# A fused attention and two-layer feed-forward kernel on one core: when the sums of x are built, by which engine, and in which slices weight blocks are converted

## Chip, cores and metric

The kernel runs on one core of a Trainium2 chip. The metric is the device time of one execution in microseconds (us). Three runs of the kernel before stand beside one profiled execution.

## What is computed

Local attention (a window of 32 positions, in half of the heads with a stride of 4) gives a matrix `x` of 2304 tokens by 512. Two feed-forward layers follow it:

```python
def reference(**kwargs):
    attn_out = _attn_ref(**attn_kwargs)          # 4 x 8 heads x 576 x 64
    x = np.ascontiguousarray(attn_out.transpose(0, 2, 1, 3)).reshape(B * S, H * D)
    x = _moe_ref(x=x, **moe_kwargs)              # silu(x @ w_gate) * (x @ w_val) @ w_out, d_ff 1536
    return _moe2_ref(x=x, **moe2_kwargs)         # ((x @ w1) * (x @ w2)) @ w3 @ w_out, d_ff 1024
```

The weights come as 64-bit floats. The kernel rebuilds 32-bit floats from their words, and splits every number into a high and a low part, so that one product is three matmuls (high by high, high by low, low by high).

## The kernel before, in words

**Slices and groups.** The two layers are cut into 20 slices `c` of 128 hidden columns: slices 0 to 11 (`NFT` = 12) are layer one, 12 to 19 layer two. In each slice the tokens are worked off in five groups `g`, four of 512 tokens and one of 256. A step (c, g) is written (8, 2) below. `steps` (L938) walks through them.

**One step.** `up_mm` (L564) forms two products into PSUM banks `pa` and `pb`, 24 matmuls. `up_act` makes `ga` of `pa` on ScalarE (L576 with SiLU in layer one, L578 a copy in layer two), `pr` = `pb` by `ga` on VectorE (L637), its high part `sh` on ScalarE (L644) and its low part `sl` on GpSimd (L645). Then comes `down` of the step *before*: 12 matmuls of `sh` and `sl` with the third weight block into banks `po0` to `po3`, and VectorE adds these to the sums `y` (L730, layer one) or `o` (L728, L730, layer two). So `sh` and `sl` of a step are wanted on TensorE one whole step after its `up` products have ended. A matmul covers 512 columns; group 4 has half the columns, or half the matmuls.

**Jobs.** What stands between two steps is set by a table, `plan(c)` (L210 on), and run by `follow` (L925). A job `("w", c+1, j)` converts weight block j of the next slice: five operations on VectorE (L126 to L136, `to_f32`), a cast on ScalarE (L199, `whi`), a subtraction on GpSimd (L200, `wlo`). `("wo", j, 0)` does the same for one of the eight blocks of the last matrix, `("w3", f, half)` for half a block of `w3`, with a transpose. `("fold", f)` is 24 matmuls that multiply `w3` and the last matrix into one matrix, which goes to memory and comes back as blocks `("fw", c, 2)`, which need a cast and a subtraction but no conversion. Loads run ahead by two jobs on SyncE's queue (`run_jobs`, L258).

**Pairs.** In the slices of `PAIRS` (L205) the groups 0 and 1 are done in one go by `pair` (L865): seven half products in place of eight, so 42 matmuls in place of 48. For that it needs four sums of blocks of `x`, and sums of weights. `t_sums` (L814) builds the former once for each layer, as a generator that does one part at each `("T",)`: additions of 128x1024 on VectorE (L816, L819), each result cast on ScalarE (`split`, L811) and its low part subtracted on GpSimd (L812). The first of them takes the place of part of `x` itself and must wait for the last plain product of group 1. `s_sums` (L855) builds the sums of weights slice by slice. The buffers of the sums of x take the room of those of the fold, so all folds come first.

**Slice 11** is the last of layer one. Its `down1` adds in another order of tokens (`total`, L751), casts the result to the next layer's `x_hi` on ScalarE (L755) and subtracts `x_lo` on GpSimd (L756), group by group, while the products of slice 11 and 12 go on.

Of the kernel before, what the change touches and what calls it, by code (L numbers as in the profile page):

```python
# [23 lines left out]
KW = QB + WINDOW  # L24
NIDLE = 8
GFILL = 4
PAIR0, PAIR1 = 9, 13
SQ = 32
NEG = -1.0e9

# [5 lines left out]
def attention_ffn_kernel(  # L36
# [14 lines left out]
    nc = tc.nc  # L51
    B, H, S, D = q.shape
# [7 lines left out]
    NFT = FF // P  # L60
    NF2 = FF2 // P
# [5 lines left out]
    while t0 < NT:  # L67
        n = min(512, NT - t0)
# [24 lines left out]
    for _ in range(NIDLE):  # L93
# [113 lines left out]
    def order_of(c):  # L207
        return ["pair", 2, 3, 4] if c in PAIRS else [0, 1, 2, 3, 4]

    def plan(c):  # L210

        res = {g: [] for g in order_of(c)[:1] + ["mid"] + order_of(c)[1:]}
        if c in PAIRS:

            res["pair"] = [("w" if c < NFT else "fw", c, 2)]
        if c + 1 == NCH:
            return res
        w0, w1, w2 = (("w", c + 1, j) for j in range(3))
        if c + 1 >= NFT:
            w2 = ("fw", c + 1, 2)  # L220
        if c == 0:

            res[4] = [w2]
        elif c < PAIR0 - 1:
            f = 2 * (c - 4)
            if f < 0:
                res[0], res[3] = [w0, w1], [w2]
                for n, g in enumerate((1, 2, 4)):
                    if 3 * c - 3 + n < NJ:
                        res[g] = [("wo", 3 * c - 3 + n, 0)]  # L230
            else:
                res = {0: [("w3", f, 1), w0], 1: [("fold", f), ("w3", f + 1, 0), w1], 2: [("w3", f + 1, 1)],
                       3: [("fold", f + 1), w2], 4: []}
            if f >= -2:
                res[4].append(("w3", f + 2, 0) if f + 2 < NF2 else ("T", c + 1))
        elif c + 1 == PAIR1 or c + 1 == PAIR0:
            res = {0: [("T",), w0], 1: [("T",), w1, ("T",)], 2: [("T",)], 3: [("S", c + 1)], 4: []}
        elif c == NFT - 1:
            res.update({"mid": [w0], 2: [w1], 4: [("T", c + 1), w2]})
        else:  # L240
            res.update({"mid": [w0], 2: [w1], 3: [("S", c + 1)]})
        return res
# [533 lines left out]
    def down(c, g):  # L776
        (down1 if c < NFT else down2)(c, g)
# [31 lines left out]
    def split(dst, t):  # L809
        hi, lo = dst  # L810
        nc.scalar.copy(out=hi, in_=t)  # L811
        nc.gpsimd.tensor_tensor(out=lo, in0=t, in1=f32(hi), op=ALU.subtract)  # L812

    def t_sums(layer):  # L814
        def sub(dst, a, b):
            nc.vector.tensor_tensor(out=dst, in0=a, in1=b, op=ALU.subtract)  # L816

        def add(dst, a, b):
            nc.vector.tensor_tensor(out=dst, in0=a, in1=b, op=ALU.add)  # L819

        if not pair_pool:
            fp.release()
            pair_pool.append(ctx.enter_context(tc.tile_pool(name="pp", bufs=1, side="right")))
        (h11, l11), (h21, l21), (h12, l12), (h22, l22) = (tuple(f32(t) for t in half(g, k))
                                                          for g in range(2) for k in range(2))
        for i in (2, 3, 4):
            xs[i] = tuple(pair_pool[0].tile([P, HK, 512], F32R, tag=f"T{i}{n}", name=f"T{i}{n}{layer}", bufs=1)
                          for n in "hl")
        t1, d = temp("Sf", f"t1_{layer}"), temp("Sh", f"d1_{layer}")
        sub(t1, h12, h11)  # L830
        sub(d, l12, l11)
        add(t1, t1, d)
        yield
        t3, d = temp("Sh", f"t3_{layer}"), temp("Sl", f"d3_{layer}")
        sub(t3, h22, h12)
        sub(d, l22, l12)
        add(t3, t3, d)
        split(xs[3], t3)
        yield
        split(half(1, 0), t1)  # L840
        yield
        t2 = temp("Sl", f"t2_{layer}")
        sub(t2, h22, t1)
        add(t2, t2, l22)
        split(xs[2], t2)
        yield
        t4 = temp("Sh", f"t4_{layer}")
        sub(t4, h21, t2)
        add(t4, t4, l21)
        split(xs[4], t4)  # L850
        yield

    ss = {}
# [11 lines left out]
    def pair(c, between):  # L865
        whi, wlo = whl[c]
        shi, slo = ss.pop(c)

        def weights(j, k):
            return tuple(w[:, j * PW + k * HK * P:j * PW + (k + 1) * HK * P] for w in (whi, wlo))  # L870

        def sums(i):
            return shi[:, i - 1], slo[:, i - 1]

        def product(pt, a, b, first, last):
            terms = [(i, j, kk) for kk in range(HK) for i, j in ((0, 0), (1, 0), (0, 1))]
# [24 lines left out]
        product(y, weights(0, 1), half(0, 1), True, True)
        gate0 = snap("ca", x)
        add(gate0, y)
        job = plan(c)["pair"]
        for _ in range(5 if job and job[0][0] != "fw" else 0):
            next(running)
        product(x, sums(2), xs[2], False, False)
        product(z, sums(1), half(1, 0), True, False)
        gate1 = snap("cb", x)
        silu(gate0)  # L910
        product(x, sums(3), xs[3], False, False)
        val1 = snap("cc", x)
        add(val1, z)
        between()
        product(x, weights(1, 1), xs[4], False, True)
        prod(0, gate0, x)
        next_job()
        product(z, sums(4), half(1, 1), False, True)
        add(gate1, z)
        silu(gate1)  # L920
        prod(1, gate1, val1)

    sums_of_x = []

    def follow(c, g):  # L925
        for what, *args in plan(c)[g]:
            if what == "fold":
                fold_mm(*args)
            elif what == "S":
                s_sums(*args)  # L930
            elif what == "T":
                if args:
                    sums_of_x.append(t_sums(*args))
                next(sums_of_x[-1])
            else:
                next_job()

# [2 lines left out]
    for n, (c, g) in enumerate(steps):  # L940
        if g == "pair":
            pair(c, lambda: down(*behind.pop()))
            behind = [(c, 0), (c, 1)]
        elif len(behind) == 2:
            gate, val = bank("pb", f"pb{c}_{g}", 2), bank("pa", f"pa{c}_{g}", 2)
            upp[c, g] = gate, val
            for j, pt in enumerate((gate, val)):
                for _ in up_product(c, g, j, pt):
                    pass
                if j == 0:  # L950
                    down(*behind.pop(0))
# [12 lines left out]
        if g != "pair":
            follow(c, g)
# [31 lines left out]
```

## Time and profile before

| | us |
|---|---|
| median of three runs (902.17 to 905.53) | 902.73 |
| the profiled execution, its own time | 902.85 |
| its span | 901.1 |
| TensorE (PE) busy | 865.7 (96%) |
| VectorE (DVE) busy | 685.4 (76%) |
| ScalarE (ACT) busy | 274.4 (30%) |
| GpSimd (POOL) busy | 367.9 (41%) |

The profiled execution lies 1.75 us over its span and 0.12 us over the median. In a timeline row stand the start in us, the duration in us (from first to last where a row merges several), the engine, the line of the kernel, the operation, output and inputs, their sizes, the count, and in brackets the idle time before it with what ended that. Matmul records follow each other in steps shorter than their durations, since matmuls are pipelined. A few matmul records are missing.

### The profile page before, as it was taken

Reading aid. Unit: us, or ns where it says so; the run is one execution under the profiler, and the core shown is the slowest. Engines: PE = TensorE matmul, PEld = TensorE weight load, DVE = VectorE, ACT = ScalarE, POOL = GpSimd, SP = SyncE. Lnnn points to the kernel's source line nnn. Section 1 sums busy time; section 2 is a strip of 40 time slices with the busy share of each in tenths; the row PEclk is TensorE's granted clock in tenths of the full one; section 3 lists DMA queues with packets and bytes.
Section 4 is the critical chain, followed back from the end, with each engine's and each line's share of the span. In section 5 each row is a group of like instructions: output and inputs, shape, how many; then the busy total and the mean of one; then the engine's idle time right before and its main releaser. Section 6 shows DMA issues by size and latency. Waiting matters only on the chain. (4 is left out here: it accounts for less than half of the span.)

```text
span 901.1 us, 13592 instructions
## 1 busy us (share of the span) xinstructions
PE 865.7 (96%) x5132; PEld 714.8 (79%) x5132; DVE 685.4 (76%) x1150; ACT 274.4 (30%) x545; POOL 367.9 (41%) x332
## 2 busy tenths in 40 slices
PE   8899999999999999999989999897999999999998
PEld 5678788888888888888868888675787888878886
DVE  6898978878888878787787777898675665756744
ACT  6778422222222222222122323332222222222221
POOL 7676523333333332322253333785343334322431
PEclk9999999999999999999989999998999999999999
DMA  8988312222233333332110111101010110110014
GB/s 193 220 194 170 119 47 71 95 71 94 73 79 87 93 84 95 82 89 82 62 44 24 47 50 33 47 13 47 1 59 12 47 39 22 58 36 23 13 46 166
DMA packets 107857, 65.91 MB, mean 73 GB/s; under 512 B 71952, under 2 KB 100880, under 8 KB 107792
## 3 DMA queue, kind: packets, MB, share of 16 engines
q1 hardware_dynamic: 107248, 64.78, 26.7%
q8 instruction: 41, 0.67, 0.3%
q10 hardware_dynamic: 544, 0.26, 0.1%
q14 instruction: 24, 0.20, 0.1%
HBM read 58.20 MB, written 6.82 MB: 72 GB/s over the span
## 5 line engine op out<-in xcount | busy, mean ns | idle before, releaser
L645 POOL TENSOR_TENSOR sl<-pr,sh 128x512 fp32r<-128x512 f32 (+1 forms) x98 | 115.6, 1180 | 171.6 <-ACT sh L644 171.6
L200 POOL TENSOR_TENSOR wlo<-val_w,whi 128x512 fp32r<-128x512 f32 x52 | 67.8, 1304 | 167.2 <-ACT whi L199 165.2
L730 DVE TENSOR_TENSOR y<-po,y 128x512 f32<-128x512 f32 (+1 forms) x200 | 114.5, 629 | 1.0 <-PE po L744 1.0
L637 DVE TENSOR_TENSOR pr<-pb,ga 128x512 f32<-128x512 f32 (+1 forms) x68 | 41.7, 613 | 96.0 <-ACT ga L576 44.3
L560 PE MATMUL pa<-x_hi,whi 128*128 128x512 f32 (+1 forms) x312 | 112.6, 364 | 0.0
L560 PE MATMUL pa<-x_hi,wlo 128*128 128x512 f32 (+1 forms) x312 | 112.3, 363 | 0.0
L560 PE MATMUL pb<-x_hi,whi 128*128 128x512 f32 (+1 forms) x312 | 112.1, 362 | 0.0
L560 PE MATMUL pb<-x_hi,wlo 128*128 128x512 f32 (+1 forms) x312 | 112.0, 362 | 0.0
L560 PE MATMUL pb<-x_lo,whi 128*128 128x512 f32 (+1 forms) x312 | 100.5, 362 | 0.0
L560 PE MATMUL pa<-x_lo,whi 128*128 128x512 f32 (+1 forms) x312 | 100.3, 362 | 0.0
L744 PE MATMUL po<-sh,whi 128*128 128x512 f32 (+1 forms) x240 | 90.3, 376 | 7.7 <-DVE total L751 3.7
L644 ACT CAST sh<-pr 128x512 fp32r<-128x512 f32 (+1 forms) x98 | 56.6, 577 | 129.0 <-DVE pr L637 79.2
L744 PE MATMUL po<-sl,whi 128*128 128x512 f32 (+1 forms) x240 | 90.8, 378 | 1.7 <-POOL sl L645 1.7
L730 DVE TENSOR_TENSOR o<-po,o 128x512 f32<-128x512 f32 x126 | 80.9, 684 | 14.0 <-PE po L771 14.0
L744 PE MATMUL po<-sh,wlo 128*128 128x512 f32 (+1 forms) x240 | 89.6, 373 | 0.0
L199 ACT CAST whi<-val_w 128x512 fp32r<-128x512 f32 x52 | 32.2, 620 | 187.6 <-DVE val_w L136 187.6
L560 PEld LDWEIGHTS pa<-x_hi,whi 128*128 128x128 f32 x312 | 59.0, 189 | 9.7
L560 PEld LDWEIGHTS pa<-x_hi,wlo 128*128 128x128 f32 x312 | 58.9, 189 | 9.6
L560 PEld LDWEIGHTS pb<-x_hi,whi 128*128 128x128 f32 x312 | 58.9, 189 | 9.2
L560 PEld LDWEIGHTS pb<-x_hi,wlo 128*128 128x128 f32 x312 | 58.9, 189 | 9.1
L560 PEld LDWEIGHTS pa<-x_lo,whi 128*128 128x128 f32 x312 | 57.4, 188 | 9.2
L560 PEld LDWEIGHTS pb<-x_lo,whi 128*128 128x128 f32 x312 | 57.5, 189 | 9.0
(182 smaller groups left out, 1821.1 us busy)
## 6 DMA issues: line engine op xcount, KB each, us to landing
raw_w<-in_moe_w_dram SPq DMA_DIRECT2D x256, 32.0 KB, 1.9
raw_w<-in_moe_w_dram SPq DMA_DIRECT2D x16, 512.0 KB, 3.5
raw_w<-in_moe_w_gate_dram SPq DMA_DIRECT2D x12, 512.0 KB, 4.0
raw_w<-in_moe_w_val_dram SPq DMA_DIRECT2D x12, 512.0 KB, 3.8
raw_w<-in_moe_w_out_dram SPq DMA_DIRECT2D x12, 512.0 KB, 3.6
out_dram<-o SPq DMA_DIRECT2D x18, 256.0 KB, 2.1
raw_wo<-in_moe_w_out_dram SPq DMA_DIRECT2D x8, 512.0 KB, 3.4
vnear<-in_v_dram SPq DMA_DIRECT2D x32, 96.0 KB, 4.8
```

Source lines behind the costliest of these rows:

```text
L199: nc.scalar.copy(out=hi, in_=val)
L200: nc.gpsimd.tensor_tensor(out=lo, in0=val, in1=hi.bitcast(F32), op=ALU.subtract)
L560: nc.tensor.matmul(out=pt[:, :n], lhsT=a[:, ws], rhs=tokens(x, kk, t0, n), start=i == 0, stop=i == len(terms) - 1)
L637: nc.vector.tensor_tensor(out=pr[:, :n], in0=pb[:, :n], in1=ga[:, :n], op=ALU.mult)
L644: nc.scalar.copy(out=sh[:, :n], in_=pr[:, :n])
L645: nc.gpsimd.tensor_tensor(out=sl[:, :n], in0=pr[:, :n], in1=sh[:, :n].bitcast(F32), op=ALU.subtract)
L730: nc.vector.tensor_tensor(out=dst, in0=src, in1=dst, op=ALU.add)
L744: nc.tensor.matmul(out=po[:, :n], lhsT=a[:, ws], rhs=x[:, :n], start=first, stop=last)
```

## The change

`PAIR1` goes from 13 to 14: slice 12 was plain before, now 12 and 13 are, and pairs run in nine slices (9 to 11, 14 to 19). The table `plan` is rewritten: all eight `wo` jobs stand in slices 1 and 2 (they stood in 1, 2 and 3), the folds with their `w3` jobs in slices 3 to 6 (4 to 7 before), and the parts of the sums of x from slice 6's last group to slice 8, in layer two from slice 12 to 13. In slice 11 the conversions stand after the pair, after group 3 and after group 4; they stood in the middle and after group 2, with the last after group 4. `t_sums` does its low parts on VectorE (`low`) in place of GpSimd, one part later than the cast (`high`), and puts the sum that replaces part of `x` last. In `pair` the job for the third block is issued earlier.

```diff
-PAIR0, PAIR1 = 9, 13
+PAIR0, PAIR1 = 9, 14
...
-        elif c < PAIR0 - 1:
-            f = 2 * (c - 4)
...
+        elif c < 3:
+
+            res[0], res[3] = [w0, w1], [w2]
+            wo = [("wo", j, 0) for j in range(NJ)]
+            if c == 1:
+                res[1], res[2], res[4] = wo[0:2], wo[2:3], wo[3:5]
             else:
...
+                res[1], res[2], res[4] = wo[5:7], wo[7:8], [("w3", 0, 0)]
...
+        elif c == PAIR0 - 2:
+            res = {0: [w0, w1], 1: [T], 2: [], 3: [w2], 4: [T]}
+        elif c == PAIR0 - 1:
+            res = {0: [T], 1: [w0, T, T], 2: [w1, T], 3: [("S", c + 1)], 4: []}
         elif c == NFT - 1:
-            res.update({"mid": [w0], 2: [w1], 4: [("T", c + 1), w2]})
+            res.update({"after": [w0], 3: [w1], 4: [w2]})
+        elif c == PAIR1 - 2:
+            res = {0: [T], 1: [w0, T], 2: [w1], 3: [w2], 4: [T]}
+        elif c == PAIR1 - 1:
+            res = {0: [w0, T], 1: [w1, T, T], 2: [T], 3: [("S", c + 1)], 4: []}
...
+        def high(i, t):
+            nc.scalar.copy(out=xs[i][0], in_=t)
+
+        def low(i, t):
+            sub(xs[i][1], t, f32(xs[i][0]))
+
...
-        split(xs[3], t3)
-        yield
-        split(half(1, 0), t1)
+        high(3, t3)
         yield
         t2 = temp("Sl", f"t2_{layer}")
         sub(t2, h22, t1)
+        low(3, t3)
         add(t2, t2, l22)
-        split(xs[2], t2)
+        high(2, t2)
         yield
...
-        split(xs[4], t4)
+        high(4, t4)
+        low(2, t2)
+        yield
+        low(4, t4)
+        yield
+
+        high(1, t1)
+        yield
+        low(1, t1)
         yield
...
-        job = plan(c)["pair"]
-        for _ in range(5 if job and job[0][0] != "fw" else 0):
-            next(running)
+        if c < NFT:
+            for _ in range(5):
+                next(running)
+        else:
+            next_job()
...
+        if c < NFT:
+            next_job()
         between()
         product(x, weights(1, 1), xs[4], False, True)
         prod(0, gate0, x)
-        next_job()
```

VectorE between `pr` of (1, 1) and `pr` of (1, 2), before; `y` is the sum that `down` of (1, 0) feeds, `val_wo` a block of the last matrix under conversion:

```order
L730 TENSOR_TENSOR y_2142<-po_0_3_2412,y_2142 128x512
L126 TENSOR_SCALAR val_wo_0_2419<-raw_wo_0_2341 128x512
L128 TENSOR_SCALAR val_wo_0_2419<-val_wo_0_2419 128x512
L130 TENSOR_SCALAR val_wo_0_2419<-val_wo_0_2419 128x512
L133 SCALAR_TENSOR_TENSOR val_wo_0_2419<-raw_wo_0_2341,val_wo_0_2419 128x512
L136 SCALAR_TENSOR_TENSOR val_wo_0_2419<-raw_wo_0_2341,val_wo_0_2419 128x512
L637 TENSOR_TENSOR pr_2_2455<-pb_2_2428,ga_2_2453 128x512
```

The same place now:

```order
L737 TENSOR_TENSOR y_2142<-po_0_3_2412,y_2142 128x512
L126 TENSOR_SCALAR val_wo_0_2419<-raw_wo_0_2341 128x512
L128 TENSOR_SCALAR val_wo_0_2419<-val_wo_0_2419 128x512
L130 TENSOR_SCALAR val_wo_0_2419<-val_wo_0_2419 128x512
L133 SCALAR_TENSOR_TENSOR val_wo_0_2419<-raw_wo_0_2341,val_wo_0_2419 128x512
L136 SCALAR_TENSOR_TENSOR val_wo_0_2419<-raw_wo_0_2341,val_wo_0_2419 128x512
L126 TENSOR_SCALAR val_wo_0_2429<-raw_wo_0_2353 128x512
L128 TENSOR_SCALAR val_wo_0_2429<-val_wo_0_2429 128x512
L130 TENSOR_SCALAR val_wo_0_2429<-val_wo_0_2429 128x512
L133 SCALAR_TENSOR_TENSOR val_wo_0_2429<-raw_wo_0_2353,val_wo_0_2429 128x512
L136 SCALAR_TENSOR_TENSOR val_wo_0_2429<-raw_wo_0_2353,val_wo_0_2429 128x512
L644 TENSOR_TENSOR pr_2_2465<-pb_2_2438,ga_2_2463 128x512
```

A second conversion stands ahead of `pr` of (1, 2). The same happens ahead of `pr` of (2, 0) and of (2, 2).

VectorE ahead of `pr` of (8, 2), before; `t` is the second of the sums of x:

```order
L126 TENSOR_SCALAR val_w_1_5315<-raw_w_1_5105 128x512
L128 TENSOR_SCALAR val_w_1_5315<-val_w_1_5315 128x512
L130 TENSOR_SCALAR val_w_1_5315<-val_w_1_5315 128x512
L133 SCALAR_TENSOR_TENSOR val_w_1_5315<-raw_w_1_5105,val_w_1_5315 128x512
L136 SCALAR_TENSOR_TENSOR val_w_1_5315<-raw_w_1_5105,val_w_1_5315 128x512
L816 TENSOR_TENSOR t_8_5323<-x_hi_70,t_8_5179 128x1024
L819 TENSOR_TENSOR t_8_5323<-t_8_5323,x_lo_75 128x1024
L637 TENSOR_TENSOR pr_2_5356<-pb_2_5329,ga_2_5354 128x512
```

The same place now; `T4l` is a low part that GpSimd made before:

```order
L126 TENSOR_SCALAR val_w_0_5310<-raw_w_0_4948 128x512
L128 TENSOR_SCALAR val_w_0_5310<-val_w_0_5310 128x512
L130 TENSOR_SCALAR val_w_0_5310<-val_w_0_5310 128x512
L133 SCALAR_TENSOR_TENSOR val_w_0_5310<-raw_w_0_4948,val_w_0_5310 128x512
L136 SCALAR_TENSOR_TENSOR val_w_0_5310<-raw_w_0_4948,val_w_0_5310 128x512
L823 TENSOR_TENSOR T4l_4876<-t_0_5249,T4h_4875 128x1024
L644 TENSOR_TENSOR pr_2_5350<-pb_2_5323,ga_2_5348 128x512
```

Two additions have gone from here to an earlier step, and one subtraction has come.

VectorE after the pair of slice 11, before; `total` and `y` are the four sums of `down` of (11, 0):

```order
L896 TENSOR_TENSOR pr_1_6218<-cc_6173,cb_6164 128x512
L751 TENSOR_TENSOR total_6242<-po_0_0_6238,y_2142 128x2x4x64
L751 TENSOR_TENSOR y_2142<-po_0_1_6246,y_2142 128x2x4x64
L751 TENSOR_TENSOR y_2142<-po_0_2_6253,y_2142 128x2x4x64
L751 TENSOR_TENSOR y_2142<-po_0_3_6260,y_2142 128x2x4x64
L126 TENSOR_SCALAR val_w_0_6269<-raw_w_0_5999 128x512
```

The same place now:

```order
L917 TENSOR_TENSOR pr_1_6218<-cc_6173,cb_6164 128x512
L126 TENSOR_SCALAR val_w_0_6226<-raw_w_0_5999 128x512
L128 TENSOR_SCALAR val_w_0_6226<-val_w_0_6226 128x512
L130 TENSOR_SCALAR val_w_0_6226<-val_w_0_6226 128x512
L133 SCALAR_TENSOR_TENSOR val_w_0_6226<-raw_w_0_5999,val_w_0_6226 128x512
L136 SCALAR_TENSOR_TENSOR val_w_0_6226<-raw_w_0_5999,val_w_0_6226 128x512
L758 TENSOR_TENSOR total_6254<-po_0_0_6250,y_2142 128x2x4x64
L758 TENSOR_TENSOR y_2142<-po_0_1_6258,y_2142 128x2x4x64
```

The conversion has moved ahead of the four sums.

## Rows read from the trace of the kernel before

**Rows 1.** Stretches: length, busy time of each engine (count), granted clock, DMA.
```profile
128.09:202.09 74.00, 74.00 (x361) 62.69 (x360) 60.62 (x107) 16.56 (x30) 25.29 (x20) 1.00 0.24 79
432.03:476.20 44.17, 40.06 (x181) 32.64 (x180) 36.14 (x46) 11.11 (x16) 17.50 (x11) 0.92 0.08 26
558.88:641.61 82.73, 69.07 (x301) 54.28 (x300) 70.34 (x75) 28.86 (x49) 56.59 (x39) 0.94 0.09 29
641.61:677.86 36.25, 36.03 (x169) 29.83 (x168) 24.62 (x43) 9.47 (x18) 14.12 (x10) 1.00 0.12 37
```

**Rows 2.** Timeline of TensorE: first matmuls of `down` after long waits.
```profile
464.64 0.77 PE L744 MATMUL po<-sh,whi 128*128 128x512 f32 x1 [3.54 <-ACT sh L644]
...
585.79 0.58 PE L744 MATMUL po<-sh,whi 128*128 128x512 f32 x1 [3.68 <-DVE total L751]
...
617.60 0.79 PE L771 MATMUL po<-whi,sh 128*128 128x512 f32 x1 [5.06 <-ACT sh L644]
...
630.30 0.47 PE L771 MATMUL po<-whi,sh 128*128 128x512 f32 x1 [1.20 <-ACT sh L644]
```

**Rows 3.** Timeline of VectorE, ScalarE and GpSimd ahead of 464.64.
```profile
450.09 0.69 DVE L637 TENSOR_TENSOR pr<-pb,ga 128x512 f32<-128x512 f32 x1 [1.29 <-ACT ga L576]
...
458.99 2.20 DVE L819 TENSOR_TENSOR t<-t,x_lo 128x1024 f32<-128x1024 f32 x1
463.20 0.69 DVE L637 TENSOR_TENSOR pr<-pb,ga 128x512 f32<-128x512 f32 x1 [2.02 <-ACT ga L576]
...
461.22 1.04 ACT L811 CAST T2h<-t 128x1024 fp32r<-128x1024 f32 x1 [2.75 <-DVE t L819]
...
452.77 2.40 POOL L812 TENSOR_TENSOR x_lo<-t,x_hi 128x1024 fp32r<-128x1024 f32 x1
```

**Rows 4.** Timeline of VectorE in slices 1 and 2.
```profile
144.20 0.69 DVE L637 TENSOR_TENSOR pr<-pb,ga 128x512 f32<-128x512 f32 x1 [1.18 <-ACT ga L576]
...
147.20 0.42 DVE L126 TENSOR_SCALAR val_wo<-raw_wo 128x512 int32<-128x512 int32 x1
...
151.18 0.69 DVE L637 TENSOR_TENSOR pr<-pb,ga 128x512 f32<-128x512 f32 x1 [1.19 <-ACT ga L576]
...
173.72 1.07 DVE L126 TENSOR_SCALAR val_w<-raw_w 128x512 int32<-128x512 int32 x1
...
182.16 0.69 DVE L637 TENSOR_TENSOR pr<-pb,ga 128x512 f32<-128x512 f32 x1 [1.18 <-ACT ga L576]
...
196.17 0.69 DVE L637 TENSOR_TENSOR pr<-pb,ga 128x512 f32<-128x512 f32 x1 [1.24 <-ACT ga L576]
```

**Rows 5.** Timeline of GpSimd and TensorE at `down` of (2, 3).
```profile
197.60 1.30 POOL L645 TENSOR_TENSOR sl<-pr,sh 128x512 fp32r<-128x512 f32 x1 [0.64 <-ACT sh L644]
...
199.35 0.40 PE L744 MATMUL po<-sh,whi 128*128 128x512 f32 x1
```

**Rows 6.** Timeline of VectorE: one addition of a sum alone, and slices 11 and 12.
```profile
433.98 1.22 DVE L816 TENSOR_TENSOR d<-x_lo,x_lo 128x1024 f32<-128x1024 f32 x1
...
578.51 1.41 DVE L128 TENSOR_SCALAR val_w<-val_w 128x512 f32<-128x512 f32 x1
...
585.75 3.55 DVE L751 TENSOR_TENSOR y<-po,y 128x512 f32<-128x512 f32 x3
...
616.15 0.69 DVE L637 TENSOR_TENSOR pr<-pb,ga 128x512 f32<-128x512 f32 x1 [1.22 <-ACT ga L578]
...
628.86 0.69 DVE L637 TENSOR_TENSOR pr<-pb,ga 128x512 f32<-128x512 f32 x1 [1.60 <-ACT ga L578]
```

**Rows 7.** Timeline of GpSimd and TensorE after the pair of slice 13.
```profile
654.22 1.74 POOL L200 TENSOR_TENSOR wlo<-raw_fw,whi 128x512 fp32r<-128x512 f32 x1
...
656.02 0.50 PE L771 MATMUL po<-wlo,sh 128*128 128x512 f32 x1 [0.22 <-POOL wlo L200]
```

**Rows 8.** Stretches as in Rows 1, around a long wait and around short ones.
```profile
457.00:471.00 14.00, 9.89 (x36) 7.46 (x35) 10.22 (x13) 4.32 (x6) 6.30 (x4) 0.76 0.13 39
624.00:641.00 17.00, 13.68 (x69) 10.77 (x68) 13.20 (x18) 5.20 (x8) 8.78 (x5) 1.00 0.10 31
```

More of the change, by code (lines that the diff above doesn't have):

```diff
@@ L210, in plan @@
     def plan(c):
-        res = {g: [] for g in order_of(c)[:1] + ["mid"] + order_of(c)[1:]}
+        T = ("T", c)
+        res = {g: [] for g in order_of(c)[:1] + ["after", "mid"] + order_of(c)[1:]}
         if c in PAIRS:
@@ L223, in plan @@
             res[4] = [w2]
-        elif c < PAIR0 - 1:
-            f = 2 * (c - 4)
[L226 to L230, printed above, removed]
-            else:
[L232 to L237, printed above, removed]
-        elif c == NFT - 1:
-            res.update({"mid": [w0], 2: [w1], 4: [("T", c + 1), w2]})
+        elif c < 3:
[3 more added lines that the diff above has]
+                res[1], res[2], res[4] = wo[0:2], wo[2:3], wo[3:5]
+            else:
+                res[1], res[2], res[4] = wo[5:7], wo[7:8], [("w3", 0, 0)]
+        elif c < 3 + NF2 // 2:
+            f = 2 * (c - 3)
+            res = {0: [("w3", f, 1), w0], 1: [("fold", f), ("w3", f + 1, 0), w1], 2: [("w3", f + 1, 1)],
+                   3: [("fold", f + 1), w2], 4: [("w3", f + 2, 0) if f + 2 < NF2 else T]}
+        elif c == PAIR0 - 2:
+            res = {0: [w0, w1], 1: [T], 2: [], 3: [w2], 4: [T]}
+        elif c == PAIR0 - 1:
+            res = {0: [T], 1: [w0, T, T], 2: [w1, T], 3: [("S", c + 1)], 4: []}
+        elif c == NFT - 1:
+            res.update({"after": [w0], 3: [w1], 4: [w2]})
[3 more added lines that the diff above has]
+            res = {0: [w0, T], 1: [w1, T, T], 2: [T], 3: [("S", c + 1)], 4: []}
         else:
@@ L825, in t_sums @@
                                                           for g in range(2) for k in range(2))
+        xs[1] = half(1, 0)
         for i in (2, 3, 4):
@@ L921, in pair @@
         prod(1, gate1, val1)
-    sums_of_x = []
+    sums_of_x = {}
     def follow(c, g):
@@ L931, in follow @@
             elif what == "T":
-                if args:
-                    sums_of_x.append(t_sums(*args))
-                next(sums_of_x[-1])
+                layer = args[0] >= NFT
+                if layer not in sums_of_x:
+                    sums_of_x[layer] = t_sums(int(layer))
+                next(sums_of_x[layer])
             else:
@@ L942, in attention_ffn_kernel @@
             pair(c, lambda: down(*behind.pop()))
+            follow(c, "after")
             behind = [(c, 0), (c, 1)]
```

## The prediction

> **What bounds the kernel now.** I read the stretches by stage first. In slices 1 and 2 TensorE is busy for all of 74.00 us at the full granted clock [rows 1], so a plain slice costs 37.0 us. A plain slice holds the work of 162 matmuls of 512 columns (4.5 groups by 36), which makes 0.228 us each. Slice 8 has the same work and takes 44.17 us, 7.17 more. The stretch from the pair of slice 11 to the end of slice 12 holds 270 matmuls, 61.7 us, and takes 82.73, so 21.1 us are lost there [rows 1]. These two places lose 28 us; elsewhere TensorE runs almost without a gap.
>
> Next I read the timeline of TensorE for who ended those waits: 3.54 us at 464.64 and 5.06 us at 617.60 by `sh`, 3.68 us at 585.79 by a sum on VectorE, 1.20 us at 630.30 by `sh` [rows 2]. Then I walked up the queues before 464.64. `sh` follows `pr` of (8, 2), which starts at 463.20, 13.1 us after the one before it at 450.09 [rows 3], while TensorE needs only 36 x 0.228 = 8.2 us for a step. Between the two, VectorE did the sums `y`, a conversion and two additions of `t_sums`, the last for 2.20 us; then ScalarE cast T2h, and `ga` and `pr` came behind that, VectorE idle for 2.02 us. An addition alone takes 1.22 us [rows 6]. The rest of 2.20 is GpSimd's: an operation of VectorE with both inputs in SBUF is late when GpSimd is at work. So VectorE's queue sets the pace in slices 8, 11 and 12, TensorE's everywhere else, and the chip answers the long waits with a clock of 1.2 GHz for some us: 0.76 granted in 457 to 471, 1.00 in 624 to 641, where the waits are short [rows 8].
>
> **The change part by part.** Each term is against the profiled execution, 902.85 us, which is 0.12 over the median.
>
> *Eight `wo` jobs in slices 1 and 2 in place of 1 to 3.* Three steps get a second conversion: ahead of `pr` of (1, 2), (2, 0) and (2, 2). VectorE is close to its limit there already. From its first operation to the next `pr` one conversion takes 151.18 - 147.20 = 3.98 us. Two take 182.16 - 173.72 = 8.44, of which 0.65 is the first operation's wait (1.07 in place of 0.42), so 7.8 [rows 4]. A second conversion costs 3.8 us. Three are 11.5. The cover is the slack of `sl`: at (2, 3) it ends at 197.60 + 1.30 = 198.90 [rows 5] (2.73 after its `pr` at 196.17, rows 4), and the second matmul wants it at 199.35 + 0.23 = 199.58, so 0.68 us are free. TensorE waits 11.5 - 0.7 = **10.8 us** in all by (2, 3), in five or six waits of 0.8 to 2.6 us. In the fold slices behind it TensorE has 24 matmuls (5.5 us) more in two steps each, and VectorE gets ahead again; nothing is given back. Lower bound: a second conversion that costs only its operations, 2.8 us (3.98 less some 1.2 of ScalarE's hand-over [rows 4]), gives 7.6. The folds, moved one slice forward, bring the work with them that was there before; nothing else is costed for them.
>
> *Sums of x in layer one.* Slices 7 and 8 share what stood in 8. VectorE gets four low parts of 1.22 us, GpSimd loses four of 2.40 (as `x_lo` in rows 3). I walked VectorE's queue from (7, 0) on: `pr` and the four sums 3.0 us, a conversion 2.8 (3.9 where it comes second), a part of `t_sums` 3.7 and 2.0 for the hand-over [rows 3, 4]. The longest steps are (7, 0) with two conversions, 10.4 us, and (7, 1), 8.7; (8, 1) with a conversion and one low part takes 8.5, (8, 2) 7.5. The lag over TensorE's 8.2 never exceeds what `sl` has in hand (least at (8, 3): ends about 1 us before it is wanted). So all of **-7.2** goes. What could be late next is (8, 3), for about 1 us, if GpSimd's `wlo` gets ahead of a low part.
>
> *Layer boundary.* Here new waits stay. In order: the conversion after the pair comes ahead of the four sums of (11, 0), which take 4.6 us (three in 3.55 [rows 6]), so `down` of (11, 1) finds its last bank late by 0.7. The conversion moved behind group 3 still runs beside GpSimd's `x_lo`, its operations of 0.43 us taking up to 1.41 [rows 6], 4.7 us in all. It ends at about 587.4 in the clock of the old trace, `wlo` 2 us later, and the second half of `up` of (12, 0) wants it at 586.9: 2.3 us. `down` of (11, 4) waits 0.85 for its banks. Ahead of (12, 2) stand a conversion and a part of `t_sums` as before, and the step took 628.86 - 616.15 = 12.7 us [rows 6] against 8.2; with the slack that I find there TensorE waits 3.1, and 1.5 once more at (12, 3). From slice 13 on no step is over its slack. Sum of new waits 8.4, so 21.1 - 8.4 = **-12.7**. Bounds: 3 us of waits if the additions meet no GpSimd work, 15 if each of the steps stays as late as now.
>
> *One pair fewer.* Slice 13 as a plain slice costs 37.0, as a pair 36.25 [rows 1]: **+0.75**.
>
> *The third block's job earlier in `pair`.* In layer two `wlo` ends at 654.22 + 1.74, and TensorE's second matmul of `down` starts 0.38 late for it, with 0.22 of that shown as a wait [rows 7]. The same stands at all seven pairs of layer two, six of which remain: 6 x 0.38 = **-2.3**. ScalarE's cast comes between two copies of the pair there and has over a microsecond of room. In layer one nothing waited for it: 0.
>
> Sum: 902.85 + 10.8 - 7.2 - 12.7 + 0.75 - 2.3 = 891.2; as the waits in slices 11 and 12 are the least certain and unforeseen ones only add, I forecast **892**.
>
> **A rule against this change.** The first row is that GpSimd needs 2.40 us for a subtraction of which VectorE's like takes 1.22 alone and 2.20 beside GpSimd [rows 3, 6]. The Trainium skill, "Perfetto Trace Analysis", section "Optimizing Scalar/DVE Operations", says that a saturated VectorE may be relieved by giving work to ScalarE or even GpSimd, and also that these two share a read port, so that it might not help. By its first half, taking work back onto the engine that sets the pace is a loss, which is the third rival below; by its second half, with which the 2.20 us agree, it costs little. The same skill, "SBUF — State Buffer", section "Who interferes with whom", calls the port an exclusive lock against a VectorE instruction with two SBUF inputs.
>
> **The rivals.** *The waits in slices 1, 2, 11 and 12 drop the clock.* For: waits of 3.5 to 5 us came with a granted clock of 0.76 over 14 us, so 3.4 us of full-speed time lost [rows 2, 8]. Against: 1.20 us left it at 1.00, and where VectorE sets the pace, a slower TensorE only uses up waits that it would have anyway. Mine are between, up to 2.6. Two drops that are not so covered give 892 + 6.8 = 899.
>
> *VectorE isn't late in slices 1 and 2*, since a second conversion fits into idle time: then 10.8 falls away, 881. Against it speaks that VectorE's only idle time there is the 1.2 us of hand-over at each `pr` [rows 4].
>
> *VectorE stays late with the low parts on it: slower.* The four low parts of 1.22, each late by one GpSimd operation (the 2.20 against 1.22), are 8.8 us a layer on the queue that TensorE waits for. If slices 7, 8, 12 and 13 lose by that what the spreading gains, the terms of 7.2 and 12.7 are both nought, and the time is 902.85 + 10.8 + 0.75 - 2.3 = 912. It decides from the point where the steps (8, 1) to (8, 3) and (13, 0) to (13, 2) take over 10 us each, against the 7 to 9 that I add up, since the slack of about 2 us is then gone after one step. Against: GpSimd has less to do there than before, 4 x 2.4 us.
>
> **How the numbers follow.** My forecast, 884 to 898, gets 0.70: its low end is 892 - 3.2 (cheap second conversions) - 5 (few waits at the boundary), its high end 892 + 6 (boundary as late as 15). The dropped clock, 896 to 903, gets 0.13, no lag at all (881) 0.10, VectorE stays late (912) 0.07. The range that should hold 8 in 10 is 884 to 900. A measurement of this kernel can tell about 0.5%, 4.5 us, from no change, so faster means under 898.2: 0.70 + 0.10 + 0.05 of the dropped clock = 0.85. Within 0.5%: the rest of the dropped clock, 0.08. Slower: 0.07.
>
> **What would show it.** In the timeline of TensorE: waits ended by `sl` or `sh` at `down` of (1, 2), (1, 3), (2, 0) to (2, 3), some 11 us in sum, where none is now; none over 1 us in slices 7 and 8, which then take 37 us each; up to 3 us at the second half of (12, 0) for `whi` or `wlo` and at (12, 2) for `sh`; pairs of layer two at 35.9 us in place of 36.25. The granted clock tells of the first rival. The forecast is wrong if slices 1 and 2 still take 37.0 each, or if slice 8 keeps a wait of 3 us.

## Result, and the profile after

The kernel after the change takes **888.56 us** (median, 887.68 to 888.97), the one before 902.83 beside it. The ratio is 0.9835, interval 0.9814 to 0.9856. The profiled execution is the shortest of the four, 887.68 us with a span of 885.9; the other spans are 886.6 to 887.2.

Busy time of the engines, from the page of the kernel after (columns: busy us, share of the span, instructions):

```profile
PE 861.3 (97%) x5138; PEld 714.1 (81%) x5138; DVE 679.4 (77%) x1151; ACT 272.5 (31%) x543; POOL 342.8 (39%) x323
```

Against the table of before GpSimd has lost 25 us and VectorE 6, although eight low parts came to it. TensorE has lost 4 of its busy time, and its mean granted clock is 0.994 where it was 0.988; the rest of the gain of 14 us is waits.

The stretches of the kernel after that answer to [rows 1] (slices 1 and 2; slice 8; a pair of layer two; and, as the last row, slice 11 after its pair with slice 12, called the boundary below), with short stretches behind waits between them. The columns are as there; the number ahead of DMA's is the granted clock:

```profile
126.79:211.68 84.89, 79.41 (x361) 64.74 (x360) 71.38 (x122) 18.32 (x32) 29.07 (x23) 0.96 0.28 85
440.89:477.89 37.00, 37.00 (x181) 31.35 (x180) 31.53 (x50) 10.49 (x16) 11.12 (x9) 1.00 0.12 39
...
679.52:715.25 35.73, 35.73 (x169) 29.90 (x168) 23.37 (x40) 8.98 (x16) 12.17 (x9) 1.00 0.12 38
...
155.00:169.00 14.00, 12.53 (x65) 10.18 (x64) 11.52 (x22) 3.09 (x7) 5.70 (x5) 1.00 0.20 67
178.00:185.00 7.00, 5.33 (x16) 3.72 (x15) 6.79 (x13) 1.23 (x2) 2.93 (x3) 0.76 0.28 87
...
589.00:596.00 7.00, 5.53 (x19) 4.31 (x20) 4.80 (x5) 4.08 (x8) 5.93 (x6) 0.76 0.23 75
...
560.57:628.85 68.28, 65.15 (x302) 53.06 (x301) 57.22 (x71) 25.56 (x46) 45.81 (x36) 0.98 0.11 36
```

Slices 1 and 2 take 84.89 us where they took 74.00, slice 8 takes 37.00 where it took 44.17, the boundary 68.28 where it took 82.73, and a pair 35.73 where it took 36.25.

The waits of TensorE in slices 1 and 2, from its timeline in the kernel after:

```profile
156.46 0.50 PE L751 MATMUL po<-sl,whi 128*128 128x512 f32 x1 [0.62 <-POOL sl L652]
163.42 0.50 PE L751 MATMUL po<-sl,whi 128*128 128x512 f32 x1 [0.85 <-POOL sl L652]
179.37 0.50 PE L751 MATMUL po<-sh,whi 128*128 128x512 f32 x1 [0.82 <-ACT sh L651]
180.72 0.50 PE L751 MATMUL po<-sl,whi 128*128 128x512 f32 x1 [0.85 <-POOL sl L652]
191.14 0.50 PE L751 MATMUL po<-sl,whi 128*128 128x512 f32 x1 [0.38 <-POOL sl L652]
200.50 0.50 PE L751 MATMUL po<-sh,whi 128*128 128x512 f32 x1 [1.12 <-ACT sh L651]
201.85 0.70 PE L751 MATMUL po<-sl,whi 128*128 128x512 f32 x1 [0.85 <-POOL sl L652]
```

Every one is a `down` that wants `sh` or `sl`. They add up to 5.5 us; the other 5.4 of the 10.9 stand as longer busy time (79.41 us against 74.00), the slow clock among it. Why `sh` and `sl` are late stands in VectorE's timeline, which answers to [rows 4]:

```profile
142.91 0.69 DVE L644 TENSOR_TENSOR pr<-pb,ga 128x512 f32<-128x512 f32 x1 [1.18 <-ACT ga L583]
...
145.91 0.41 DVE L126 TENSOR_SCALAR val_wo<-raw_wo 128x512 int32<-128x512 int32 x1
...
148.62 0.42 DVE L126 TENSOR_SCALAR val_wo<-raw_wo 128x512 int32<-128x512 int32 x1
...
149.53 1.48 DVE L130 TENSOR_SCALAR val_wo<-val_wo 128x512 int32<-128x512 int32 x1
...
153.65 0.69 DVE L644 TENSOR_TENSOR pr<-pb,ga 128x512 f32<-128x512 f32 x1 [1.18 <-ACT ga L583]
```

Two conversions stand between two `pr`. The step takes 153.65 - 142.91 = 10.74 us where it took 6.98 [rows 4], 3.76 more, and VectorE is idle in it for the hand-over of 1.18 us alone. The first conversion takes 148.62 - 145.91 = 2.71 us. The second takes 1.05 more, since its third operation (L130) needs 1.48 us and not 0.43. GpSimd subtracts the first block's low part at that moment, and ScalarE's rows show what the hand-over is:

```profile
149.43 1.29 POOL L200 TENSOR_TENSOR wo_lo<-val_wo,wo_hi 128x512 fp32r<-128x512 f32 x1 [3.75 <-ACT wo_hi L199]
...
152.50 0.62 ACT L199 CAST wo_hi<-val_wo 128x512 fp32r<-128x512 f32 x1 [3.14 <-DVE val_wo L136]
153.03 0.59 ACT L583 ACTIVATE ga<-pa 128x512 f32<-128x512 f32 x1
```

The last matmul into this `pa` ends at 144.7 in TensorE's timeline. `ga` comes only at 153.03 because the cast of the second block stands ahead of it in ScalarE's queue, and that waits for VectorE's conversion.

At the boundary, TensorE's waits:

```profile
589.62 0.50 PE L567 MATMUL pb<-x_hi,whi 128*128 128x512 f32 x1 [0.79 <-ACT whi L199]
590.97 0.70 PE L567 MATMUL pb<-x_hi,wlo 128*128 128x512 f32 x1 [0.85 <-POOL wlo L200]
...
619.41 0.50 PE L778 MATMUL po<-whi,sl 128*128 128x512 f32 x1 [0.40 <-POOL sl L652]
...
625.11 0.47 PE L778 MATMUL po<-whi,sh 128*128 128x512 f32 x1 [0.25 <-ACT sh L651]
626.43 0.50 PE L778 MATMUL po<-whi,sl 128*128 128x512 f32 x1 [0.62 <-POOL sl L652]
```

The waits of 3.68 and 5.06 us [rows 2] have gone. What stays is the second half of `up` of (12, 0), which waits for its weights, and some tenths at (12, 2) and (12, 3).

### The profile page after: what moved, and what is told of

It reads as the page before. It is cut to its first block, busy times and chain, and to the rows that moved or that the text cites. A ratio compares the mean times of both kernels' runs of the same rounds, so it can differ in the third digit from the quotient of the medians.

```text
span 885.9 us, 13578 instructions
## 1 busy us (share of the span) xinstructions
PE 861.3 (97%) x5138; PEld 714.1 (81%) x5138; DVE 679.4 (77%) x1151; ACT 272.5 (31%) x543; POOL 342.8 (39%) x323
## 4 chain that ended last, share of the span: by engine, by line
PE 73%; DVE 19%; issue 3%; POOL 2%; ACT 2%; DMA 1%; SPq 0%; ACTq 0%; DVEq 0%; POOLq 0%
PE pa L567 17%; PE pb L567 17%; PE po L751 13%; PE po L778 10%; PE px L899 6%; PE fold L792 5%; PE pz L899 3%; DVE y L737 2%; PE py L899 1%; DVE val_w L130 1%; DVE y L758 1%; DVE val_w L133 1%; DVE mx L473 1%; DVE s L467 1%; DVE val_w L128 1%
## 5 line engine op out<-in xcount | busy, mean ns | idle before, releaser
L567 PE MATMUL pb<-x_hi,wlo 128*128 128x512 f32 (+1 forms) x320 | 116.0, 365 | 0.9 <-POOL wlo L200 0.9
L567 PE MATMUL pb<-x_hi,whi 128*128 128x512 f32 (+1 forms) x320 | 116.0, 365 | 0.8 <-ACT whi L199 0.8
L644 DVE TENSOR_TENSOR pr<-pb,ga 128x512 f32<-128x512 f32 (+1 forms) x71 | 43.7, 616 | 94.9 <-ACT ga L583 40.3
L567 PE MATMUL pa<-x_hi,whi 128*128 128x512 f32 (+1 forms) x320 | 115.6, 364 | 0.0
L567 PE MATMUL pa<-x_hi,wlo 128*128 128x512 f32 (+1 forms) x320 | 115.4, 363 | 0.0
L567 PE MATMUL pb<-x_lo,whi 128*128 128x512 f32 (+1 forms) x320 | 103.8, 365 | 0.0
L567 PE MATMUL pa<-x_lo,whi 128*128 128x512 f32 (+1 forms) x320 | 103.0, 363 | 0.0
L567 PEld LDWEIGHTS pb<-x_hi,whi 128*128 128x128 f32 x320 | 60.8, 190 | 10.8 <-ACT whi L199 1.2
L567 PEld LDWEIGHTS pb<-x_hi,wlo 128*128 128x128 f32 x320 | 60.8, 190 | 10.7 <-POOL wlo L200 1.2
L567 PEld LDWEIGHTS pb<-x_lo,whi 128*128 128x128 f32 x320 | 59.3, 190 | 9.4
```

Source lines behind the costliest of these rows:

```text
L567: nc.tensor.matmul(out=pt[:, :n], lhsT=a[:, ws], rhs=tokens(x, kk, t0, n), start=i == 0, stop=i == len(terms) - 1)
L644: nc.vector.tensor_tensor(out=pr[:, :n], in0=pb[:, :n], in1=ga[:, :n], op=ALU.mult)
```

## Experiments

Times are medians; the kernel before took 902.3 to 903.2 beside them. "After" is 888.56.

**The second conversions left out.** In slices 1 and 2 a `wo` block that comes second in its step is not converted on VectorE; its cast and subtraction read the first one's result.

```diff
-            val = wp.tile([P, PW], F32, tag="wval", name=f"val_{kind}{a}_{j}", bufs=2)
-            yield from to_f32(val, raw_of.pop(job))
+            if kind == "wo" and a in (1, 4, 6):
+                val = last_wo[0]
+                raw_of.pop(job)
...
```

> The changed kernel, but the second conversion of a step that the change put into slices 1 and 2 (blocks 1, 4 and 6 of the last matrix) does nothing on VectorE: ScalarE and GpSimd split the value of the block before it again, so three blocks of the last matrix are wrong. Theory (VectorE's queue sets the pace there): the 10.9 us that slices 1 and 2 take over 74.0 go, steps (1, 1), (1, 4), (2, 1) fall from 10.5 to 10.7 us to about 7; 888.6 - 10.9 = 877.7 us. Rival (the waits come with the blocks' loads, casts or GpSimd work, which stay): at least 884 us.

Measured: 878.93 (ratio 0.9737, 0.9722 to 0.9751). The stretch of slices 1 and 2, with the same columns as above:

```profile
127.30:202.42 75.12, 74.57 (x362) 62.59 (x361) 60.29 (x107) 18.03 (x32) 28.93 (x23) 1.00 0.30 96
```

The two slices take 9.8 us less, at full clock. Fifteen operations of VectorE, 10.6 us of its busy time (679.4 to 668.8 on the two pages), were worth 9.6 us of the kernel. So the price of slices 1 and 2 is VectorE's queue. The loads, casts and subtractions of the three blocks stayed, and only 1.1 us over the 74.00 of before is left. GpSimd has a part in the price all the same, by the 1.05 us that each second conversion takes longer beside its subtraction.

**Low parts on GpSimd again.**

```diff
-            sub(xs[i][1], t, f32(xs[i][0]))
+            nc.gpsimd.tensor_tensor(out=xs[i][1], in0=t, in1=f32(xs[i][0]), op=ALU.subtract)
```

> The changed kernel with the four low parts of the sums of x on GpSimd again, all else as it is. Theory (the spreading brings the gain, not the engine): VectorE has 4.9 us less to do in each layer, in steps that have slack anyway, so 888.6 us within 1.5; slices 7 and 8 keep 37.0 us each. Rival (the low parts beside GpSimd's work are what made VectorE late): over 892 us, with waits for sh in slice 8 or 12. Second rival (a saturated VectorE is relieved by it): the waits at (12, 2) and (12, 3), 2 us, go, under 887 us.

Measured: 890.39 (0.9867, 0.9850 to 0.9883), just over the theory's upper end and under the rival's 892. A wait at (8, 3) comes back; it, and the stretches of slice 8 and of the boundary:

```profile
477.86 0.50 PE L751 MATMUL po<-sl,whi 128*128 128x512 f32 x1 [0.95 <-POOL sl L652]
...
442.26:480.49 38.23, 37.27 (x182) 31.33 (x181) 29.76 (x42) 9.95 (x15) 18.86 (x13) 1.00 0.11 35
563.16:631.47 68.31, 64.07 (x301) 51.88 (x300) 57.24 (x71) 25.58 (x46) 46.33 (x37) 1.00 0.11 36
```

The choice of the engine is worth 1.8 us by the medians. By the rows it is 1.2 us in slice 8 and nothing at the boundary. The spread over two slices, which this kernel keeps, holds the rest: slice 8 takes 38.23 us where it took 44.17.

**Low parts on VectorE, nothing else.** The kernel before with the new `t_sums` and its parts where the sums stood before, in slice 8 and in slice 12.

```diff
-            res = {0: [("T",), w0], 1: [("T",), w1, ("T",)], 2: [("T",)], 3: [("S", c + 1)], 4: []}
+            res = {0: [("T",), w0], 1: [("T",), w1, ("T",)], 2: [("T",), ("T",), ("T",)], 3: [("S", c + 1)], 4: []}
...
```

> The kernel before with the low parts of the sums of x on VectorE, but all sums within the slice where they stood (8 and 12), nothing else changed. Theory (the spreading brings the gain, not the engine): VectorE has 4.9 us more in each of two slices in which it sets the pace, GpSimd 9.6 less; the long waits stay, 902.8 us and up to 8 more. Rival (GpSimd's hold on the port was the cause): under 895 us, with slice 8 near 40 us.

Measured: 901.08 (0.9975, 0.9964 to 0.9987). TensorE's long waits in it, and the stretch of slice 8:

```profile
462.91 0.47 PE L744 MATMUL po<-sh,whi 128*128 128x512 f32 x1 [2.79 <-ACT sh L644]
...
583.59 0.76 PE L744 MATMUL po<-sh,whi 128*128 128x512 f32 x1 [3.67 <-DVE total L751]
...
613.37 0.50 PE L771 MATMUL po<-whi,sh 128*128 128x512 f32 x1 [2.84 <-ACT sh L644]
...
627.52 0.48 PE L771 MATMUL po<-whi,sh 128*128 128x512 f32 x1 [3.44 <-ACT sh L644]
...
431.31:473.96 42.65, 39.01 (x181) 32.38 (x180) 37.59 (x53) 11.65 (x17) 9.49 (x7) 0.96 0.09 27
```

The waits of [rows 2] are all there: 5.06 us has become 2.84, but 1.20 has become 3.44. The engine alone gives some 2 us (903.17 beside it), about what undoing it costs above; 1.5 of it is in slice 8. The theory had no gain at all, so its range was missed on the lower side, and the rival's 895 was not reached.

**The pair's job late again.** It goes back behind `prod(0, gate0, x)`, as before the change: in layer two the whole job, in layer one its cast and its subtraction.

```diff
-        if c < NFT:
-            for _ in range(5):
-                next(running)
-        else:
-            next_job()
+        for _ in range(5 if c < NFT else 0):
+            next(running)
...
-        if c < NFT:
-            next_job()
...
+        next_job()
```

> The changed kernel with the third block's job in the pair put back behind the first product of pr. Theory: the pairs of layer two take 36.25 us again in place of 35.74, six times 0.51, so 888.6 + 3.1 = 891.7 us. Rival (the cast moved only shifts ScalarE's work, and the 0.5 comes from elsewhere): within 1 us of 888.6.

Measured: 892.69 (0.9891, 0.9876 to 0.9905). The first of six waits that answer to [rows 7], one in each pair of layer two:

```profile
681.73 0.50 PE L778 MATMUL po<-wlo,sh 128*128 128x512 f32 x1 [0.23 <-POOL wlo L200]
```

The pairs of layer two are 36.25 us apart again, against 35.73 in after. This part is worth 4.1 us by the medians, of which the six pairs explain 3.1. The other 1.0 lies in layer one, in the pair of slice 11. The second `pr` of that pair in after, and then in this run with GpSimd beside it:

```profile
562.23 0.69 DVE L917 TENSOR_TENSOR pr<-cc,cb 128x512 f32<-128x512 f32 x1 [0.77 <-POOL sl L652]
```

```profile
562.75 1.72 DVE L917 TENSOR_TENSOR pr<-cc,cb 128x512 f32<-128x512 f32 x1 [0.77 <-POOL sl L652]
...
562.63 1.30 POOL L200 TENSOR_TENSOR wlo<-val_w,whi 128x512 fp32r<-128x512 f32 x1
```

The late `wlo` of the third block runs beside this `pr`, which takes 1.03 us longer. VectorE sets the pace behind it, and the boundary takes 69.33 us (561.09 to 630.42) in place of 68.28.

**The conversions of slice 11 at their old places.**

```diff
-            res.update({"after": [w0], 3: [w1], 4: [w2]})
+            res.update({"mid": [w0], 2: [w1], 4: [w2]})
```

> The changed kernel with slice 11's conversions where they were before: the first after the four sums of (11, 0), the second after group 2, the third after group 4. Theory: the wait of 3.7 us at down of (11, 3) with its slow clock comes back (some 6 us in all from 565 to 592), the waits at (11, 1) and at the second half of up of (12, 0) go (4.9 us); 889.7 us, between 888 and 892. Rival (the moved conversions are the main gain at the boundary): over 895 us.

Measured: 890.96 (0.9872, 0.9857 to 0.9886). TensorE's timeline shows the wait of [rows 2] again:

```profile
589.17 0.47 PE L751 MATMUL po<-sh,whi 128*128 128x512 f32 x1 [3.69 <-DVE total L758]
```

In return the wait at (12, 2) is gone. The move is worth 2.4 us, within the theory's bounds: it gives up one wait of 3.7 for shorter ones.

**Folds later.** The `wo` jobs in slices 1 to 3 as before, folds in 4 to 7, sums of x in 8 and 9, pairs from slice 10.

```diff
-PAIR0, PAIR1 = 9, 14
+PAIR0, PAIR1 = 10, 14
...
-        elif c < 3:
+        elif c < 4:
...
+            for n, g in enumerate((1, 2, 4)):
+                if 3 * c - 3 + n < NJ:
+                    res[g] = [("wo", 3 * c - 3 + n, 0)]
...
-            f = 2 * (c - 3)
+            f = 2 * (c - 4)
```

> The changed kernel with the blocks of the last matrix in slices 1 to 3 and the folds in slices 4 to 7 as before, the sums of x of layer one in slices 8 and 9, and so one pair fewer (10, 11, 14 to 19). Theory: the 10.9 us of slices 1 and 2 go, 0.9 of short waits in slices 3 and 4 come back, slice 9 costs 37.0 in place of 35.8; 888.6 - 10.9 + 0.9 + 1.2 = 879.8 us. Rival (VectorE's lag turns up elsewhere): 885 us or more.

Measured: **879.68** (0.9745, 0.9729 to 0.9761). Slices 1 and 2 in its stretches:

```profile
126.00:200.00 74.00, 74.00 (x362) 62.69 (x361) 60.77 (x108) 16.48 (x29) 25.85 (x21) 1.00 0.24 79
```

74.00 us and full clock, as before. The 10.9 us are bought back with one pair fewer and with the short losses that the kernel before had in slices 3 and 4. By the starts of the slices in TensorE's timeline, slice 9 takes 37.00 us in place of 35.78, and slices 3 and 4 lose 0.8. That leaves 10.9 - 1.2 - 0.8 = 8.9, which is what the medians differ by.

**Conversions at the boundary one place earlier.** The third block of slice 11 behind (10, 4), the first of slice 12 in the pair of 11, the second behind the pair.

```diff
+        if c == NFT - 2:
+            res[4] = [("w", c + 1, 2)]
+        if c == NFT - 1:
+            res["pair"] = [("w", c + 1, 0)]
...
-            res.update({"after": [w0], 3: [w1], 4: [w2]})
+            res.update({"after": [w1], 4: [w2]})
...
```

> The changed kernel with the conversions of slices 10 and 11 each one place earlier: the third block of slice 11 after group 4 of slice 10, the first block of slice 12 in the pair of slice 11, the second after it, none after group 3. Theory: the wait at the second half of up of (12, 0) with its slow clock goes (3.9 us), and VectorE comes into slice 12 nearly 5 us earlier, so the 2.0 us at (12, 2) and (12, 3) go too; 888.6 - 5.5 = 883 us. Rival (the lag moves to down of (11, 1) or to the pair of slice 11): 887 us or more.

Measured: 889.27 (0.9849, 0.9834 to 0.9864); together with the later folds, 879.62 (0.9744, 0.9730 to 0.9759):

> Folds later and the boundary's conversions earlier, both. Theory: the two gains stand in different slices and add up: 888.6 - 8.8 - 5.5 = 874.3 us. Rival (they overlap): 878 us or more.

The theory fell in both, and the rivals held. The wait at (12, 0) has gone, but a new one stands in the pair of slice 11; the waits at (12, 2) and (12, 3), which the theory also had go, stay in the first of the two (0.63, 0.24 and 0.61). TensorE and ScalarE around the new wait, from the timeline of the first of the two:

```profile
556.23 0.50 PE L903 MATMUL px<-T2h,Sh 128*128 128x512 f32 x1 [2.84 <-ACT ca L909]
...
555.07 0.62 ACT L199 CAST whi<-val_w 128x512 fp32r<-128x512 f32 x1 [4.69 <-DVE val_w L136]
555.60 0.58 ACT L909 COPY ca<-px 128x512 f32<-128x512 f32 x1
```

The cast of the converted block stands ahead of the copy `ca` in ScalarE's queue and waits 4.69 us for VectorE. TensorE may not add to `px` before `ca` has copied it.

**The third block another step earlier**, behind the weight sums after (10, 3), with the later folds (set against the run of both):

```diff
-        if c == NFT - 2:
-            res[4] = [("w", c + 1, 2)]
...
+        elif c == NFT - 2:
+            res.update({"mid": [w0], 2: [w1], 3: [("S", c + 1), ("w", c + 1, 2)]})
```

> Folds later as in the run of the later folds, and at the boundary as in the run of the earlier conversions, except for one place: the third block of slice 11 is converted behind the weight sums after group 3 of slice 10, no longer behind group 4. Theory: the new wait of 2.7 to 3.0 us in the pair of slice 11 came because the cast of that block (ScalarE, waiting for VectorE's conversion) stood in ScalarE's queue ahead of the copy ca of px, which TensorE's next product into px waits for. With the conversion done one step earlier the cast is long over when px ends, the wait at 545 to 556 is gone, and the wait at the second half of (12, 0) stays gone: 879.6 - 2.7 = 877, or down to 875 if the slow clock at the boundary goes too. Rival: the copy ca is late for another reason (VectorE's sums y of the steps before, or the added step ahead of pr of (10, 4), which makes down late there): then a wait of over 2 us stays between 535 and 556 and the time is 879 or more.

Measured: **877.37** (0.9719, 0.9701 to 0.9738), the fastest of all. TensorE and ScalarE at the same place, and the stretch of the boundary:

```profile
546.44 0.50 PE L903 MATMUL px<-T2h,Sh 128*128 128x512 f32 x1 [1.58 <-ACT ca L909]
...
544.05 0.62 ACT L199 CAST whi<-val_w 128x512 fp32r<-128x512 f32 x1 [3.79 <-DVE val_w L136]
...
545.50 0.41 ACT L655 CAST sh<-pr 128x256 fp32r<-128x256 f32 x1 [0.54 <-DVE pr L648]
545.81 0.58 ACT L909 COPY ca<-px 128x512 f32<-128x512 f32 x1
...
554.96:618.67 63.71, 62.74 (x301) 52.06 (x300) 52.79 (x66) 25.04 (x45) 44.19 (x35) 1.00 0.10 30
```

Each account was half right, and the time is the theory's 877. The weights' cast no longer stands directly ahead of `ca`, but the conversion now makes `pr` of (10, 4) late, and `sh` of that step stands ahead of `ca` instead: 1.58 us are left, as the rival's second branch says, and under its bound of 2. At (12, 0) there is no wait, and the boundary takes 63.71 us in place of 68.28, at full clock.

## Why the prediction was right, and where its terms were off

The forecast was 892.0 with a range of 884 to 900; 888.56 lies in it, 3.4 us lower. The sum in the prediction is added up wrongly: its terms give 892.2 and not 891.2, so 892 was the bare sum, with nothing added for unforeseen waits. Term by term, measured in the two profiled executions:

| term | predicted | measured |
|---|---|---|
| slices 1 and 2 | +10.8 | 84.89 - 74.00 = +10.9 |
| slice 8, with 7 | -7.2 | 37.00 - 44.17 = -7.2 |
| slice 11 after its pair, slice 12 | -12.7 | 68.28 - 82.73 = -14.5 |
| slice 13 a plain one | +0.75 | 36.90 - 36.25 = +0.65 |
| six pairs of layer two | -2.3 | 6 x (35.73 - 36.25) = -3.1 |
| not in the sum | 0 | -2.0 |

The measured terms sum to -15.2, and the profiled run is 902.85 - 887.68 = 15.2 us shorter. Of the last line 0.7 us are slices 3 to 7, which took 229.94 us (202.09 to 432.03) and take 229.21 (211.68 to 440.89). The other 1.3 lie ahead of slice 1, in the attention part, which the change doesn't touch. They belong to this run and not to the change: `pr` of (1, 1) starts at 142.91 in it, and between 143.4 and 144.7 in the other ten profiled runs, the kernel before among them.

**Slices 1 and 2** went as worked out: a second conversion costs 10.74 - 6.98 = 3.76 us (3.8 in the sum), three of them less the slack. The lower bound, the operations alone, misses the 1.05 us that the second conversion loses beside GpSimd. The first experiment removed just these operations and got 9.6 us back, and the later folds 8.9 with one pair fewer. The rival in which a second conversion fits into idle time is refuted. The sign was half right: waits of some 11 us were forecast, and 5.5 us of waits and 5.4 of slower matmuls came.

**Slices 7 and 8** have no wait in the rows, and slice 8 takes 37.00 us, as forecast. From `pr` to `pr` VectorE's timeline has 7.97 us for (8, 1) and 7.36 for (8, 2), where 8.5 and 7.5 were added up. That this is mostly the spreading and not the engine is shown by slice 8 in the pair of experiments: 38.23 us with the spread alone, 42.65 with the engine alone, 44.17 with neither.

**The boundary** had its right places, and one wrong size. Its losses are read from the starts of TensorE's steps, each against the same step without a wait: 0.7 us at `down` of (11, 1) as forecast (566.01 to 572.17, 6.16 us where slice 10 has 5.44); 3.8 at (12, 0) where 2.3 + 0.85 = 3.15 were (587.4 + 2 - 586.9, the figures given, make 2.5 of the 2.3); 0.7 at (12, 2) where 3.1 were; 1.4 at (12, 3) where 1.5 were. They sum to 6.6 in place of 8.4. The step that failed is the slack ahead of (12, 2). From `pr` to `pr` the step is nearly as long as I had it:

```profile
604.64 0.68 DVE L644 TENSOR_TENSOR pr<-pb,ga 128x512 f32<-128x512 f32 x1
...
616.65 0.69 DVE L644 TENSOR_TENSOR pr<-pb,ga 128x512 f32<-128x512 f32 x1 [1.60 <-ACT ga L585]
```

It takes 12.01 us where I had the 12.7 of [rows 6]; that is 0.7 of the 2.4 us by which (12, 2) was overpriced. At (12, 0) TensorE needs 10.66 us for `up` of (12, 0) and `down` of (11, 4), which hold 24 x 0.228 + 12 x 0.114 = 6.8; the 3.8 lost are the two waits shown and a slow clock behind them, in place of the wait for banks that I expected. That delay gives slack downstream. In the run with the pair's job late the clock stayed at full speed there. The steps of (12, 0) and (12, 2), first in after and then in that run:

```profile
585.95:596.61 10.66, 9.02 (x37) 6.99 (x36) 7.66 (x9) 4.75 (x9) 7.77 (x7) 0.84 0.15 49
612.96:621.83 8.87, 8.47 (x38) 6.68 (x36) 7.10 (x12) 2.15 (x3) 1.29 (x1) 1.00 0.03 11
```

```profile
587.52:596.97 9.45, 7.68 (x38) 5.91 (x36) 7.55 (x9) 3.66 (x7) 6.58 (x6) 1.00 0.16 55
613.32:623.39 10.07, 8.70 (x38) 6.60 (x36) 8.30 (x12) 2.15 (x3) 2.25 (x2) 1.00 0.14 49
```

The two steps take 19.53 and 19.52 us in sum: what the slow clock costs at (12, 0), 1.2 us, comes back at (12, 2). So 1.2 of the 2.4 is this delay; I had added the two waits up as if each stood alone. The last 0.5 is the slack that I took without a row. That the term came out only 1.8 us off is in part luck, since (12, 0) was underpriced by 0.65.

**The pairs** have got 0.52 us shorter where I had 0.38, the second matmul's delay in [rows 7]. What the other 0.14 are, the rows don't tell. That the job's place is the cause, undoing it shows. The prediction put the job's place in layer one at 0, since nothing waited for `wlo` there; that step is wrong. What is at stake is not a wait for `wlo` but `pr` of (11, 1), which runs beside it when the job is late. Undoing the move makes 1.7 us of the 0.7 at `down` of (11, 1).

**The rivals.** The clock did fall, twice in slices 1 and 2 and once at (12, 0). It cost next to nothing. In the two runs in which it stayed at full speed at (12, 0), with the low parts on GpSimd and with the pair's job late, it also fell once less in slices 1 and 2, and these take 84.72 us there (128.10 to 212.82, 127.25 to 211.97) against 84.89. VectorE sets the pace in both places, and TensorE's slower matmuls filled what would have been waiting. So the second argument against that rival held, and not the first: drops came behind waits of 0.82 and 0.85 us. The rival in which the low parts keep VectorE late is refuted in general, not only for this plan: without the spread they gave some 2 us and not a loss of 8.8. The step of it that fails is a price of one GpSimd operation for each low part. All eight take 1.21 to 1.22 us in after, as if alone; one of them:

```profile
643.44 1.21 DVE L823 TENSOR_TENSOR T2l<-t,T2h 128x1024 fp32r<-128x1024 f32 x1
```

By that the Trainium skill's advice to relieve a saturated VectorE with GpSimd ("Perfetto Trace Analysis", section "Optimizing Scalar/DVE Operations") would have lost here, where undoing the move to VectorE cost 1.8 us; its warning on the shared port, in the same section, is the half that the trace agrees with (1.72 us against 0.69 for the `pr` beside GpSimd's `wlo`).

**What stays open.** Whether the last 1.58 us in the pair of slice 11 can go: no run tried the third block behind group 2. And whether the hand-over of 1.18 us at each `pr` can go: no run issued `ga` ahead of the cast that it stands behind.

## What to carry to other kernels

Where one engine's queue feeds TensorE step by step, add up that queue for each step, hand-over included, against TensorE's step: work is free in steps that stay under it and costs its full length in steps that are at it, so the same jobs over three slices cost 0.8 us at most and over two cost 10.9. Spreading a burst was worth far more here than choosing the engine that runs it. Two slow steps in a row need not add up: here a delay of TensorE at the first was slack at the second. When an operation is moved to an earlier place, look at every in-order queue that it passes, not only at the engine that is short of time: here a cast that waited for VectorE blocked a copy that TensorE needed, and gave back all of the gain.

## What the runs showed of the hardware

**The clock does not follow the lengths of the waits alone.** In after, waits of 0.82 and 0.85 us, which end 1.35 us apart at 179 to 181, brought the granted clock from 2.4 to 1.2 GHz for some us (0.76 in 178 to 185), as did 0.79 and 0.85 at 590. Two single waits of 0.62 and 0.85 left it at full speed (155 to 169), and so had 1.20 and 1.07 us in the kernel before (624 to 641 at 1.00 [rows 8]). But the same pair of waits can end either way: at (12, 0) 0.79 and 0.85 us, again 1.35 us apart, left the clock at 1.00 in the run with the pair's job late (587.52 to 596.97, shown above). Waits for `ca` at one and the same place ended in both ways. The stretches behind them, of the early conversions alone (2.84 us) and then with the later folds (2.50 us):

```profile
553.00:570.00 17.00, 14.16 (x68) 11.55 (x67) 12.21 (x22) 5.31 (x9) 5.16 (x4) 1.00 0.16 47
```

```profile
545.00:552.00 7.00, 4.50 (x14) 3.40 (x13) 4.85 (x9) 2.22 (x4) 1.27 (x1) 0.76 0.16 37
```

The longer wait kept the full clock, the shorter one lost it. So a drop could not be forecast from these lengths; what it costs could, from whether TensorE is the engine that sets the pace there.

**GpSimd's work lengthens operations of VectorE, and not only those with two inputs in SBUF**, of which the prediction speaks. `pr` of two SBUF tensors took 1.72 us beside a subtraction on GpSimd and 0.69 without one; the third operation of a conversion, which reads one tensor, took 1.48 beside one and 0.43 without. Of the first three operations of the conversions between 130 and 740 us in after, none of the 152 without work of GpSimd beside them took over 0.6 us, and 25 of the 40 with it did.
